# Attention on TensorE with another order of work inside a pair of heads, and the last 64 keys handled at full height

## The chip, the cores and the metric

One core of one Trainium2 chip runs the whole program. The metric is the device time of an execution in microseconds (us). The engines are named as in the profile: PE (TensorE matmul; PEld is its weight load), DVE (VectorE), ACT (ScalarE), POOL (GpSimd) and SP (SyncE, which here only issues DMA transfers).

## The reference, cut to what matters

Block-causal attention over 8 batches of 8 heads (576 positions, head size 64, blocks of 64), and then a mixture of 8 experts in which each of the 4608 tokens goes to its best expert alone.

```python
scores = scale * np.matmul(q, k.transpose(0, 1, 3, 2))
mask = block_i >= block_j                      # blocks of 64 positions
scores = np.where(mask, scores, -1000000000.0)
scores = scores - np.max(scores, axis=-1, keepdims=True)
attn = np.exp(scores)
attn = attn / (np.sum(attn, axis=-1, keepdims=True) + 1e-09)
x = np.matmul(attn, v)                         # to (4608, 512)
...
e_idx = np.argmax(x @ w_gate, axis=1)
for e in range(E):
    h = np.maximum(x[mask] @ w1[e], 0.0)
    out[mask] = gate_w[mask, None] * eom[mask, e, None] * (h @ w2[e])
```

## The kernel before

**Pairs.** Attention goes through 32 pairs of heads, p = 0 to 31; a batch is four pairs, and a unit of loading (u) is two pairs. In each round of the loop `advance(PLAN, p, ...)` three pairs are in flight. For pair p the softmax part runs: scores S0 to S4 on PE, one for each query tile (S0 to S3 are tiles of 128 queries, S4 the last 64 queries of both heads), their row maxima M0 to M4 on DVE, and the exponentials E0A to E4 on ACT, which also add up the row sums. For pair p-1 the probabilities are transposed: F0 to F5 are four fp32 transposes of 128x128 each on PE into a tile of `ps_t`, F6 is that of the last 64 keys, and C0 to C6 copy them to `pT` on ACT. For pair p-2 the values are multiplied in: V0 and V1 (the first 512 queries, into `ps_a`) and VM (the last 64 queries, into `ps_t`) on PE, X and XM copy the results to `xT` on ACT.

**What sets the order.** `PLAN` is a list of these names, written by hand, and each engine gets its instructions in the order of the list. PE keeps that order in all pairs; DVE and ACT keep it in pairs 1 to 27, and from pair 28 on a scheduler orders these two. A name with "-" (X-, E4-) is a piece that was left over from the round before. A "|" ends a turn: there the generators in `later` go one step on, which are the loads of the units to come, the finishing of a batch (`finish_batch`: reciprocals of the sums, the expert logits on PE, DVE and ACT, the routing tables) and `load_first` (the first expert's weights, from pair 28 on). Both lists have eight turns.

**Scores and their buffers.** The scores of tiles 0 and 1 of a pair share one buffer of `ps_s`, those of tiles 2, 3 and 4 take one each, and `ps_s` has two buffers. So S1 and S0 can start when the buffer of S3 has been read by E3A and E3B, S2 when that of S4 has been read by E4, S3 when that of S1 and S0 has been read by E1 and E0, S4 when E2 has read that of S2. `ps_t` has three buffers, `ps_a` one. In the list S0 stands behind M1, the maximum that DVE reads from the buffer into which S0 writes.

**The last 64 keys.** F6 transposes columns 512 to 575 of the last query tile's probabilities alone, to 64 rows; VM multiplies them by `v8`, the last 64 rows of V of both heads, as a product of height 64, behind four products of height 128.

**Loads.** A unit's q and k are fetched, split into two fp16 parts on POOL (`split`), transposed by two DMA transfers from SP's queue (`turn`), and then half swapped by two copies on DVE (`swap`, L115). Counted in turns from the start of the generator, `turn` comes at 8 and 9 and `swap` at 18 and 20, which for most units is in the pair just ahead of their first use. The last unit (15) is first used in pair 30; its generator starts in pair 26, one pair earlier than those of the others, and its `swap` comes at 13 and 14, in pair 27.

After pair 31 the mixture of experts runs, some 400 us of it, and the change does not touch it.

Of the kernel before, what the change touches and what calls it, by code (L numbers as in the profile page):

```python
# [20 lines left out]
P = 128  # L21
# [5 lines left out]
def block_attention_top1_moe(  # L27
# [56 lines left out]
    class Load:  # L84
# [26 lines left out]
        def swap(self, half):  # L111
            if half == 0:
                self.sw = sb.tile([P, MAXH * S], F16, name="sw")
            to, of = slice(64 * half, 64 * half + 64), slice(64 - 64 * half, 128 - 64 * half)
            nc.vector.tensor_copy(self.sw[to], self.res[0][of])  # L115

        def done(self):
            loaded[self.u] = (self.res[1], self.res[0], self.sw)

    def load_heads(u):  # L120

        x = Load(u)
        for i in range(2 if u == 2 else 0):
# [4 lines left out]
            lambda: x.turn(0), lambda: x.turn(1), lambda: x.swap(0), lambda: x.swap(1),  # L128
        )
        at = 0  # L130
        for t, do in zip((4, 5, 8, 9) + ((13, 14) if u == len(units) - 1 else (18, 20)), todo):
            while at < t:
                at += 1
                yield
            do()
        x.done()
# [5 lines left out]
    def load_start():  # L142
# [75 lines left out]
        nxt.turn(1)  # L218
        nxt.swap(0)
        nxt.swap(1)  # L220
        nxt.done()


    with tc.high_priority(offset=3000):
# [50 lines left out]
        nc.gpsimd.memset(wg_bd, 0.0)  # L275

# [6 lines left out]
    def constants():  # L283
# [15 lines left out]
        X- F0 S1 E4- M1 S0 | | C0 F1 F2 S2 M0 | C1 C2 E1A F4 M2 E1B E0A F3 E0B C4 C3 |  # L299
        V0 S3 F5 | E2A M3 E2B | VM C5 S4 XM E3A F6 E3B V1 | C6 M4 |  # L300
# [27 lines left out]
    def load_v(b, hp):  # L328
# [6 lines left out]
        v8 = sb.tile([64, 2, D], F32, name="v8", bufs=3)  # L335
        nc.sync.dma_start(v8, v[b, hA:hA + 2, 512:576, :].rearrange("h s d -> s h d"))
# [86 lines left out]
    def flip(probs, pT, copy):  # L423
# [31 lines left out]
        def turn_end():  # L455
            held[6] = ps_t.tile([P, 512], F32, name="ps_t")[0:64, 0:P]
            nc.tensor.transpose(held[6], probs[LAST][:, 512:S], ident)

        parts = {"F6": turn_end, "C6": lambda: copy(pT[0:64, 8 * TS:8 * TS + P], held[6])}
# [5 lines left out]
    def values(hp, pT, vs, v8, xT, copy):  # L465
# [651 lines left out]
    for p in range(B * NP):  # L1117
# [8 lines left out]
        while u not in loaded:  # L1126
            next(loads[2 * u - (4 if u == len(units) - 1 else 3)] if u else start, None)
# [34 lines left out]
    TAIL = " ".join(PLAN).replace("V1", "V1 X").split()  # L1162
# [115 lines left out]
```

## Time and profile before

| what | value |
|---|---|
| median of 3 runs | 828.63 us (830.1, 828.63, 825.52) |
| the profiled execution's own time | 818.4 us |
| its span | 816.7 us |
| PE busy | 750.4 us (92%) |
| DVE, ACT busy | 536.3 us (66%), 534.7 us (65%) |
| POOL busy | 320.5 us (39%) |

Shares of busy time are means over the program. The attention part reaches from the start to some 410 us and the experts' part from there to the end, so the stretches in the attention part have to be read by themselves.

### The profile page before, as it was taken

To read this page: it belongs to the slowest core of one execution; us is meant where nothing else is said; L and a number is where in the kernel's file an instruction comes from. 1 tells how busy PE (TensorE), PEld (TensorE's weight loads), DVE (VectorE), ACT (ScalarE), POOL (GpSimd) and SP (SyncE) were. 2 spreads that over 40 slices of the span, in tenths; PEclk is the share of its full clock that TensorE was granted. 3 is DMA by queue.
4 is the path that set the end of the run, shared out by engine and by line. 5 is a ranking of instruction groups with operands and counts; after the bars stand their busy time and mean duration, and the time that the engine had idled before them with its cause. 6 is when DMAs were issued, how large, how long until landed. Compare 5 with 4: busy or idle time off the path is not lost. (4 is left out here: it accounts for less than half of the span.)

```text
span 816.7 us, 18658 instructions
## 1 busy us (share of the span) xinstructions
PE 750.4 (92%) x6898; PEld 522.7 (64%) x6918; DVE 536.3 (66%) x1073; ACT 534.7 (65%) x1183; POOL 320.5 (39%) x445
## 2 busy tenths in 40 slices
PE   6799998999999998597979999999999999999994
PEld 3566666656666665465666775966669666686652
DVE  6556776767576776666563695867769676796530
ACT  4788787787878786576512686856568655785530
POOL 5668264463445460257224642322322243210001
PEclk9999999999999999898989999999999999999998
DMA  7889698957766365654117599699999969931601
GB/s 168 177 184 201 170 196 135 199 118 197 122 173 129 91 121 130 90 183 127 39 59 263 153 258 297 210 281 311 325 297 355 343 161 303 246 88 40 231 30 42
DMA packets 256629, 147.87 MB, mean 181 GB/s; under 512 B 224144, under 2 KB 224208, under 8 KB 256528
## 3 DMA queue, kind: packets, MB, share of 16 engines
q1 hardware_dynamic: 248416, 127.30, 60.7%
q0 software_dynamic: 8112, 19.29, 7.6%
q8 instruction: 56, 0.92, 0.5%
q14 instruction: 45, 0.37, 0.2%
HBM read 126.03 MB, written 19.34 MB: 178 GB/s over the span
## 5 line engine op out<-in xcount | busy, mean ns | idle before, releaser
L1009 PEld LDWEIGHTS <-w1b 128*128 128x128 f16 (+1 forms) x2208 | 177.7, 98 | 22.9 <-DVE w1b L886 1.3
L1009 PE MATMUL ps_s<-xt,w1b 128*128 128x256 f16 (+5 forms) x1920 | 175.2, 253 | 0.3 <-DVE w1b L886 0.3
L410 ACT ACTIVATE pt<-ps_s,nbs 128x512 f32<-128x512 f32 (+4 forms) x282 | 155.3, 569 | 17.2 <-DVE nbs L403 9.5
L1038 PE MATMUL ps_t<-w2b,hh 128*128 128x512 f16 (+1 forms) x540 | 162.4, 379 | 0.0
L395 DVE TENSOR_REDUCE nmx<-ps_s 128x2 f32<-128x1024 f32 (+1 forms) x125 | 102.9, 824 | 77.0 <-PE ps_s L380 76.4
L886 DVE TENSOR_TENSOR w2b<-w2f,w2b 128x1024 bf16<-128x1024 f32 x80 | 92.9, 1220 | 89.2 <-ACT w2b L884 88.9
L453 ACT COPY pT<-ps_t 128x512 f32<-128x512 f32 x181 | 102.2, 602 | 41.6 <-PE ps_t L444 41.6
L444 PE MATMUL ps_t<-ident,pt 128*128 128x128 f32 x768 | 112.0, 284 | 0.5 <-DVE xn L555 0.3
L1047 POOL DMA_INDIRECT out_dram<-ys,ids x38 | 49.6, 1306 | 160.0 <-ACT ys L1046 81.2
L1038 PE MATMUL ps_t<-w2b,hl 128*128 128x512 f16 x280 | 106.1, 379 | 1.1
L378 PE MATMUL ps_s<-tr,tr 128*128 128x512 f16 (+1 forms) x250 | 73.6, 307 | 35.8 <-DVE nmx L395 25.0
L1046 ACT ACTIVATE ys<-ps_t,ids 128x512 f32<-128x512 f32 (+1 forms) x38 | 26.1, 686 | 112.6 <-PE ps_t L1038 93.9
L444 PEld LDWEIGHTS ps_t<-ident,pt 128*128 128x128 f32 x768 | 85.9, 144 | 15.2 <-issue 4.3
L1038 PEld LDWEIGHTS <-hh 128*128 128x128 f16 x560 | 54.4, 98 | 62.0 <-issue 0.8
L886 DVE TENSOR_TENSOR w1b<-w1f,w1b 128x1024 bf16<-128x1024 f32 x80 | 92.8, 1217 | 1.4 <-ACT w1b L884 1.4
L103 POOL TENSOR_TENSOR sp<-nat,sp 128x320 f16<-128x320 f32 x120 | 87.5, 750 | 5.2 <-DVE sp L102 3.7
L102 POOL CAST sp<-nat 128x320 f16<-128x320 f32 x112 | 46.0, 438 | 97.4 <-DMA tr<-sp 82.2
L884 ACT CAST w1b<-w1f 128x1024 f16<-128x1024 f32 x80 | 78.3, 1045 | 2.6 <-DMA w1f<-in_moe_w_dram 2.6
L884 ACT CAST w2b<-w2f 128x1024 f16<-128x1024 f32 x80 | 77.8, 1043 | 1.5 <-DMA w2f<-in_moe_w_dram 1.5
L479 PE MATMUL ps_a<-pT,va 128*64 128x384 f32 (+2 forms) x256 | 74.6, 414 | 0.0
L479 PE MATMUL ps_a<-pT,vb 128*64 128x384 f32 (+2 forms) x256 | 74.6, 414 | 0.0
L379 PE MATMUL ps_s<-sw,tr 128*128 128x512 f16 (+1 forms) x250 | 73.4, 306 | 1.1 <-DVE sw L203 1.1
(218 smaller groups left out, 1181.8 us busy)
## 6 DMA issues: line engine op xcount, KB each, us to landing
w1f<-in_moe_w_dram SPq DMA_DIRECT2D x80, 512.0 KB
w2f<-in_moe_w_dram SPq DMA_DIRECT2D x80, 512.0 KB
nat<-in_k_dram SPq DMA_DIRECT2D x15, 576.0 KB
nat<-in_q_dram SPq DMA_DIRECT2D x15, 576.0 KB
x_d<-xn SPq DMA_DIRECT2D x32, 256.0 KB
va<-in_v_dram SPq DMA_DIRECT2D x32, 128.0 KB
vb<-in_v_dram SPq DMA_DIRECT2D x32, 128.0 KB
hh<-in_moe_w_dram SPq DMA_DIRECT2D x4, 512.0 KB
```

What stands on the lines that cost most here:

```text
L103: last_lo[0] = lo.tensor_tensor(sp[:, sl, 1, :], self.nats[i][:, sl], sp[:, sl, 0, :], ALU.subtract)
L378: nc.tensor.matmul(o, qq, k1[ab][:, 0:n], start=True, stop=False)
L379: nc.tensor.matmul(o, qq, k2[ab][:, 0:n], start=False, stop=False)
L395: nc.vector.tensor_reduce(nmx[:, t, :], at[t], AX.X, ALU.max, negate=True)
L410: last_exp[0] = nc.scalar.activation(probs[t][:, ab * n:(ab + 1) * n], at[t, ab], AF.Exp, bias=nbs[:, t, ab:ab + 1], scale=SCALE, accum_ou ...
L444: nc.tensor.transpose(held[i][:, P * j:P * j + P], probs[t][:, sl], ident)
L453: copy(to, ps)
L479: nc.tensor.matmul(pa[half, c0:512], vs[a][:, j, :], rows[:, a, j, c0 - P:512 - P], start=(j == 0), stop=(j == 3))
L884: nc.scalar.copy(hi, src)
L886: eng.tensor_tensor(lo[at], src[at], hi[at], ALU.subtract)
L1009: nc.tensor.matmul(ph[:, f4].rearrange("p (h n) -> p h n", n=w), wv[:, cc, f, :], xv[:, cc], start=(k == 0), stop=(k == 3 * KD - 1))
L1038: nc.tensor.matmul(py, hv[:, f, h], wv[:, f, :], start=(k == 0), stop=(k == 3 * KF - 1))
```

## The change

It has three parts.

1. `PLAN` is another list. On PE, S0 now follows S1 at once and M1 comes behind both; S2 comes behind F1 and F2 as before; F3 stands ahead of F4; F6 stands ahead of F5; V1 comes ahead of S4, and VM is last. On ACT, C0 comes ahead of the E4 of the pair before; C5 and C6 stand side by side ahead of E3; X and XM come last, in the round of their own values. The tail uses the same list as it is.
2. The last 64 keys are taken at full height: F6 transposes columns 448 to 575 (128x128, as the other transposes), C6 copies 128 rows, and `v8` has 128 rows, of which the upper 64 are zeros (written once, at the start, in three constant tiles that are used in turn), so that the last product of VM has height 128 as the others.
3. The last unit's swaps come at 18 and 20 like those of the others, which is in pair 28; the buffer of the swapped copy is taken with the second transpose; where a unit had to be loaded ahead of its pair by force, there is an assertion now.

```diff
     PLAN = """
-        X- F0 S1 E4- M1 S0 | | C0 F1 F2 S2 M0 | C1 C2 E1A F4 M2 E1B E0A F3 E0B C4 C3 |
-        V0 S3 F5 | E2A M3 E2B | VM C5 S4 XM E3A F6 E3B V1 | C6 M4 |
+        F0 S1 S0 M1 C0 | | E4- F1 C1 F2 M0 C2 E1A E1B E0A S2 E0B | F3 F4 C3 V0 S3 C4 |
+        M2 F6 F5 E2A E2B M3 | C5 C6 V1 S4 VM | E3A E3B X M4 | | XM
     """.split()
...
-    TAIL = " ".join(PLAN).replace("V1", "V1 X").split()
+    TAIL = list(PLAN)
...
+        v8s = [const.tile([P, 2, D], F32, name=f"v8{i}") for i in range(3)]
+        for v8 in v8s:
+            nc.gpsimd.memset(v8[0:64], 0.0)
...
-        v8 = sb.tile([64, 2, D], F32, name="v8", bufs=3)
-        nc.sync.dma_start(v8, v[b, hA:hA + 2, 512:576, :].rearrange("h s d -> s h d"))
+        v8 = v8s[(b * NP + hp) % 3]
+        nc.sync.dma_start(v8[64:128], v[b, hA:hA + 2, 512:576, :].rearrange("h s d -> s h d"))
...
-            held[6] = ps_t.tile([P, 512], F32, name="ps_t")[0:64, 0:P]
-            nc.tensor.transpose(held[6], probs[LAST][:, 512:S], ident)
+            held[6] = ps_t.tile([P, 512], F32, name="ps_t")[:, 0:P]
+            nc.tensor.transpose(held[6], probs[LAST][:, S - P:S], ident)
...
-        parts = {"F6": turn_end, "C6": lambda: copy(pT[0:64, 8 * TS:8 * TS + P], held[6])}
+        parts = {"F6": turn_end, "C6": lambda: copy(pT[:, 8 * TS:8 * TS + P], held[6])}
...
-                    if j < 4:
-                        nc.tensor.matmul(o, vs[a][:, j, :], rows[:, a, j, 512 - P:TS], start=(j == 0), stop=False)
-                    else:
-                        nc.tensor.matmul(o, v8[:, a, :], pT[0:64, 8 * TS + 64 * a:8 * TS + 64 * a + 64], start=False, stop=True)
+                    w, x = (vs[a][:, j, :], rows[:, a, j, 512 - P:TS]) if j < 4 else (v8[:, a, :], pT[:, 8 * TS + 64 * a:8 * TS + 64 * a + 64])
+                    nc.tensor.matmul(o, w, x, start=(j == 0), stop=(j == 4))
...
-        for t, do in zip((4, 5, 8, 9) + ((13, 14) if u == len(units) - 1 else (18, 20)), todo):
+        for t, do in zip((4, 5, 8, 9, 18, 20), todo):
...
-            lambda: x.turn(0), lambda: x.turn(1), lambda: x.swap(0), lambda: x.swap(1),
+            lambda: x.turn(0), lambda: (x.turn(1), x.done()), lambda: x.swap(0), lambda: x.swap(1),
...
-        while u not in loaded:
-            next(loads[2 * u - (4 if u == len(units) - 1 else 3)] if u else start, None)
+        assert u in loaded
```

**PE, the head of a pair.** L378 to L380 are a score's two products and its mask. Before, from the second half of S1 to S0:

```order
L378 MATMUL ps_s<-tr_2231,tr_2240 128x256
L379 LDWEIGHTS tr_2240
L379 MATMUL ps_s<-sw,tr_2240 128x256
L380 LDWEIGHTS mrow
L380 MATMUL ps_s<-mneg,mrow 128x64
L378 LDWEIGHTS tr_2240
L378 MATMUL ps_s<-tr_2231,tr_2240 128x128 [waits DVE_49]
L379 LDWEIGHTS tr_2240
L379 MATMUL ps_s<-sw,tr_2240 128x128
L380 LDWEIGHTS mrow
L380 MATMUL ps_s<-mneg,mrow 128x64
```

Now, the same place in the changed kernel, where the lines are L379 to L381:

```order
L379 MATMUL ps_s<-tr_2224,tr_2233 128x256
L380 LDWEIGHTS tr_2233
L380 MATMUL ps_s<-sw,tr_2233 128x256
L381 LDWEIGHTS mrow
L381 MATMUL ps_s<-mneg,mrow 128x64
L379 LDWEIGHTS tr_2233
L379 MATMUL ps_s<-tr_2224,tr_2233 128x128
L380 LDWEIGHTS tr_2233
L380 MATMUL ps_s<-sw,tr_2233 128x128
L381 LDWEIGHTS mrow
L381 MATMUL ps_s<-mneg,mrow 128x64
```

The first product of S0 (128x128) waited for DVE, that is for M1; it now waits for nothing, since M1 comes behind it.

**PE, the last keys.** L387 (L388) is S4, L457 (L458) F6, L444 (L445) the other transposes, L479 (L480) V1, and L549 a transpose of a batch's finishing. Before, from the end of S4:

```order
L387 MATMUL ps_s<-sw,tr_2240 64x64
L387 LDWEIGHTS tr_2240
L387 MATMUL ps_s<-sw,tr_2240 64x64
L457 MATMUL ps_t<-ident,pt_2738 64x128 [waits Activation_49]
L479 MATMUL ps_a<-pT,va 64x384
L479 MATMUL ps_a<-pT,vb 64x384
```

Now, from the end of S3 (L381 is its mask):

```order
L381 MATMUL ps_s<-mneg,mrow 128x64
L458 MATMUL ps_t<-ident,pt_2760 128x128 [waits DVE_49]
L445 MATMUL ps_t<-ident,pt_2760 128x128 [waits Activation_49]
L445 MATMUL ps_t<-ident,pt_2760 128x128 x3
L549 MATMUL ps_t<-ident,xT 128x128 [waits Activation_49]
L549 MATMUL ps_t<-ident,xT 128x128 x3
L480 MATMUL ps_a<-pT,va 64x384
L480 MATMUL ps_a<-pT,vb 64x384
```

F6 stood alone between S4 and V1, 64 rows high in its result; it now is 128 rows high and stands ahead of F5's four transposes, behind S3.

**ACT, from the end of one pair to the start of the next.** L410 (L411) are the exponentials, by their width: 512 is E3, 576 E4, 256 E1; L453 (L454) and L459 (L460) are the copies C0 to C5 and C6, and L493 (L492) X and XM. Before:

```order
L410 ACTIVATE pt_920,sums<-ps_s,nbs 128x512 [waits DVE_49] x2
L459 COPY pT<-ps_t 64x128 [waits PE_49]
L493 COPY xT<-ps_a 128x512 [waits PE_49]
L410 ACTIVATE pt_956,sums<-ps_s,nbs 128x576 [waits DVE_49,Activation_49]
L453 COPY pT<-ps_t 128x2x2x128 [waits PE_49,Activation_49]
L453 COPY pT<-ps_t 128x4x128 [waits PE_49] x2
L410 ACTIVATE pt_996,sums<-ps_s,nbs 128x256 [waits DVE_49]
```

Now:

```order
L411 ACTIVATE pt_931,sums<-ps_s,nbs 128x512 [waits DVE_49]
L492 COPY xT<-ps_a 128x512 [waits PE_49]
L492 COPY xT<-ps_t 128x64 [waits PE_49]
L454 COPY pT<-ps_t 128x2x2x128 [waits PE_49,Activation_49]
L411 ACTIVATE pt_972,sums<-ps_s,nbs 128x576 [waits DVE_49]
L454 COPY pT<-ps_t 128x4x128 [waits PE_49] x2
L411 ACTIVATE pt_989,sums<-ps_s,nbs 128x256 [waits DVE_49]
```

X stood ahead of E4 and now stands, with XM, behind E3 and ahead of C0, and E4 behind C0; C6 has 128 rows (and stands ahead of these rows, behind C5).

**DVE, around the last unit's swaps.** L115 (L113) are the two swaps, L395 (L396) the maxima M0 to M3 and L399 (L400) M4. Before:

```order
L453 COPY pT<-ps_t 128x2x2x128 [waits PE_49]
L395 TENSOR_REDUCE nmx<-ps_s 128x2 [waits PE_49]
L403 TENSOR_SCALAR nbs<-nmx 128x1 [waits DVE_49]
L403 TENSOR_SCALAR nbs<-nmx 128x1
L115 COPY sw<-tr_4981 64x2304 [waits DMAHW1_49]
L115 COPY sw<-tr_4981 64x2304
L399 TENSOR_REDUCE nmx<-ps_s 128x1
L687 COPY cnt_5178<-ps_t 128x8 [waits PE_49]
L403 TENSOR_SCALAR nbs<-nmx 128x1 [waits DVE_49]
L395 TENSOR_REDUCE nmx<-ps_s 128x2
```

Now:

```order
L396 TENSOR_REDUCE nmx<-ps_s 128x2
L703 SCALAR_TENSOR_TENSOR f_eq<-cnt_5153,f_mx,erev 128x8 [waits DVE_49]
L404 TENSOR_SCALAR nbs<-nmx 128x1 [waits DVE_49]
L404 TENSOR_SCALAR nbs<-nmx 128x1
L705 TENSOR_REDUCE f_er<-f_eq 128x1 [waits DVE_49]
L113 COPY sw<-tr_4960 64x2304 [waits DMAHW0_49]
L706 TENSOR_SCALAR first<-erev,f_er 128x8 [waits DVE_49]
L708 TENSOR_SCALAR f_e<-f_er 128x1
L396 TENSOR_REDUCE nmx<-ps_s 128x2 [waits PE_49]
L709 CAST f_i<-f_e 128x1 [waits DVE_49]
L113 COPY sw<-tr_4960 64x2304
```

The swaps stood right behind M1 of pair 28, ahead of M4 of the pair before (L399) and of M0; now they stand behind both, on either side of M2.

## Rows read from the trace of the kernel before

**Rows 1.** The page's first part: busy time, share of the span and instructions of each engine.

```profile
PE 750.4 (92%) x6898; PEld 522.7 (64%) x6918; DVE 536.3 (66%) x1073; ACT 534.7 (65%) x1183; POOL 320.5 (39%) x445
```

**Rows 2.** Two stretches of the attention part: start:end in us, length, then busy us and instructions of PE, PEld, DVE, ACT and POOL, the granted clock, the DMA engines' share and GB/s.

```profile
100.00:200.00 100.00, 91.97 (x935) 65.14 (x933) 70.63 (x195) 77.57 (x241) 49.79 (x85) 1.00 0.81 169
200.00:300.00 100.00, 92.73 (x939) 64.20 (x936) 69.07 (x194) 79.11 (x244) 51.03 (x88) 1.00 0.65 136
```

**Rows 3.** What PE waited for over the whole span: engine, its tile and line, the releaser, its tile and line: us in total, times, longest us.

```profile
PE ps_s L378 <- DVE nmx L395: 25.0, 31, 1.0
PE ps_s L378 <- ACT pt L410: 10.8, 8, 7.0
...
PE ps_t L564 <- ACT lgT L544: 4.0, 3, 2.6
```

**Rows 4.** The timeline of PE in pair 17, from its S1 to the S1 of pair 18: start us, us, engine, line, operation, tiles, shape of the tile of the array that is used and of the operands, count, and in brackets the idle time before it and its releaser. Matmuls overlap, so what a step costs is read from the starts. L378 to L380 at width 256, 128, 384 and 512 are S1, S0, S2 and S3, L387 is S4; L444 are the transposes F0 to F5, L457 is F6; L487 and L489 are VM, L479 V1.

```profile
205.91 0.27 PE L378 MATMUL ps_s<-tr,tr 128*128 128x256 f16 x1
...
206.37 0.19 PE L380 MATMUL ps_s<-mneg,mrow 128*128 128x64 bf16 x1
207.35 0.22 PE L378 MATMUL ps_s<-tr,tr 128*128 128x128 f16 x1 [0.78 <-DVE nmx L395]
...
207.63 1.07 PE L444 MATMUL ps_t<-ident,pt 128*128 128x128 f32 x8
208.53 0.33 PE L378 MATMUL ps_s<-tr,tr 128*128 128x384 f16 x1
...
211.27 0.39 PE L378 MATMUL ps_s<-tr,tr 128*128 128x512 f16 x1
...
212.17 0.19 PE L380 MATMUL ps_s<-mneg,mrow 128*128 128x64 bf16 x1
212.20 0.64 PE L444 MATMUL ps_t<-ident,pt 128*128 128x128 f32 x4
...
213.16 0.22 PE L487 MATMUL ps_t<-pT,va 128*64 128x64 f32 x1
...
213.22 0.22 PE L487 MATMUL ps_t<-pT,va 128*64 128x64 f32 x1
...
213.38 0.33 PE L489 MATMUL ps_t<-pT,v 64*64 64x64 f32 x4
213.64 0.41 PE L387 MATMUL ps_s<-tr,tr 128*64 128x512 f16 x2
...
214.12 0.20 PE L387 MATMUL ps_s<-sw,tr 128*64 128x64 f16 x2
214.25 0.30 PE L457 MATMUL ps_t<-ident,pt 128*64 128x128 f32 x1
214.48 0.54 PE L479 MATMUL ps_a<-pT,va 128*64 128x384 f32 x1
...
215.93 0.66 PE L444 MATMUL ps_t<-ident,pt 128*128 128x128 f32 x4
216.42 0.27 PE L378 MATMUL ps_s<-tr,tr 128*128 128x256 f16 x1
```

**Rows 5.** The timeline of ACT in the same pair: E4 of the pair before, the copies C1 and C2, E1A, and the copies C4 and C3.

```profile
206.04 0.75 ACT L410 ACTIVATE pt<-ps_s,nbs 128x576 f32<-128x576 f32 x1
...
208.30 1.08 ACT L453 COPY pT<-ps_t 128x512 f32<-128x512 f32 x2 [0.85 <-PE ps_t L444]
209.26 0.49 ACT L410 ACTIVATE pt<-ps_s,nbs 128x256 f32<-128x256 f32 x1
...
210.85 1.10 ACT L453 COPY pT<-ps_t 128x512 f32<-128x512 f32 x2
```

**Rows 6.** The timeline of DVE in the same pair, M1 alone.

```profile
206.60 0.69 DVE L395 TENSOR_REDUCE nmx<-ps_s 128x2 f32<-128x512 f32 x1 [1.14 <-PE ps_s L380]
```

**Rows 7.** Timelines of four engines: on PE the S1 of pairs 1, 28 and 29 and the S2 of pair 28, on DVE M1's last step in pair 28 and the last unit's two swaps (L115), on ACT the E4 behind them, and on SP the two transposes that the swaps wait for.

```profile
22.69 0.27 PE L378 MATMUL ps_s<-tr,tr 128*128 128x256 f16 x1 [0.69 <-ACT pt L410]
...
334.20 5.18 SPq L108 DMA_TRANSPOSE tr<-sp  x2
...
336.21 0.27 PE L378 MATMUL ps_s<-tr,tr 128*128 128x256 f16 x1
...
337.74 0.21 DVE L403 TENSOR_SCALAR nbs<-nmx 128x1 f32<-128x1 f32 x2
342.78 1.52 DVE L115 COPY sw<-tr 64x2304 f16<-64x2304 f16 x2 [4.83 <-DMA tr<-sp]
...
345.30 0.74 ACT L410 ACTIVATE pt<-ps_s,nbs 128x576 f32<-128x576 f32 x1 [5.43 <-DVE nbs L403]
...
346.18 0.48 PE L378 MATMUL ps_s<-tr,tr 128*128 128x384 f16 x1 [7.05 <-ACT pt L410]
...
356.27 0.27 PE L378 MATMUL ps_s<-tr,tr 128*128 128x256 f16 x1
```

**Rows 8.** PE's logits in pair 30, from the timeline, and the stretch around them, from the table of stretches (columns as in rows 2).

```profile
372.71 1.12 PE L564 MATMUL ps_t<-ident,lgT 128*128 128x128 f32 x4 [2.63 <-ACT lgT L544]
...
371.00:376.00 5.00, 3.29 (x15) 2.89 (x16) 1.38 (x2) 3.67 (x13) 5.00 (x9) 0.53 0.82 227
```

More of the change, by code (lines that the diff above doesn't have):

```diff
@@ L111, in swap @@
         def swap(self, half):
-            if half == 0:
-                self.sw = sb.tile([P, MAXH * S], F16, name="sw")
             to, of = slice(64 * half, 64 * half + 64), slice(64 - 64 * half, 128 - 64 * half)
@@ L117, in done @@
         def done(self):
+            self.sw = sb.tile([P, MAXH * S], F16, name="sw")
             loaded[self.u] = (self.res[1], self.res[0], self.sw)
@@ L135, in load_heads @@
             do()
-        x.done()
     units = [(b, h0, 4) for b in range(B) for h0 in (0, 4)]
@@ L218, in load_start @@
         nxt.turn(1)
+        nxt.done()
         nxt.swap(0)
         nxt.swap(1)
-        nxt.done()
     with tc.high_priority(offset=3000):
```

## The prediction

> **What bounds the kernel now.** I read the busy shares by stretch first. Over the program PE is busy 92% and ACT and DVE 65% [rows 1]; inside the attention part, from 100 to 300 us, it is PE 92 to 93%, ACT 78 to 79%, DVE 69 to 71% [rows 2]. So PE is the bound there, with some 7 to 8 us of idle in each 100 us and little else to take away. Next I read what PE waited for: one line stands out, the first score product waiting for the maximum (line L395), 25.0 us in 31 waits, 0.8 us each, and then one single wait of 7.0 us for an exponential [rows 3]. The 31 waits are one a pair. The timeline of pair 17 shows the place [rows 4]: S1 starts at 205.91, its last product at 206.37, and S0 at 207.35, 0.78 us of it idle until DVE has finished M1, which takes 0.69 us from 206.60 [rows 4, 6]. S0 writes into the buffer that M1 reads. The pair ends with the next S1 at 216.42, so it lasts 10.51 us. From pair 1 to pair 28, S1 to S1, it is (336.21 - 22.69) / 27 = 11.61 us [rows 7]; the 1.10 us above pair 17 are the finishing steps of batches that share the engines. The experts' part isn't touched, so all of the change lies in the first 410 us.
>
> **The sum** is made for the profiled execution (818.4 us) and then put on the median.
>
> (a) **S0 ahead of M1.** Before, S0's first product came 207.35 - 206.37 = 0.98 us behind S1's last; where nothing waits, a last score product is followed after 0.03 us (212.17 to 212.20) [rows 4]. That is 0.95 us a pair, and pairs 1 to 27 have it: 27 x 0.95 = 25.6 us off. (All waits of this line sum to 25.0 us as idle time, which is the modelled end's lower reading [rows 3].) The wait can go only if nothing else comes as late. What is late next, counted from S1 = 0 with the durations of pair 17: S0 ends at 0.48 + 0.28, F1 and F2 take 0.90, so PE wants S2 at 1.66, and S3 2.74 us later, at 4.40 [rows 4]. S2 needs the buffer that E4 of the pair before reads. ACT now does C0 first: F0 ends at about 0.17 (215.93 + 0.66 against 216.42), C0 takes half of the 0.96 us of two copies, so E4 starts near 0.68; in pair 28, S2 started 0.88 us behind E4 [rows 4, 5, 7]. That gives 1.56: free by 0.10 us. S3 needs E0B: E4 0.75, two copies 0.96, E1 and E0 together 210.85 - 209.26 = 1.59, so it ends near 4.0 and S3 may go at 4.2, free by 0.2 us [rows 5]. M1, which now starts behind S0, at about 0.97, is followed by E1 only at 2.4, so its 0.69 us are covered by E4 and the copies. S4 needs E2, done near 6.1, and PE comes to S4 at about 7.35: free by 1.2 us. The margins at S2 and S3 are thin, and this is the first rival below.
>
> (b) **The last keys at full height, and the new neighbours on PE.** The last ordinary product of VM comes at 213.22, one pair of products lasts 213.22 - 213.16 = 0.06, the half-height ones come at 213.38 and S4 at 213.64 [rows 4]. In one shape the way from 213.22 to 213.64 would be three steps of 0.06, not 0.42: about 0.25 us less. S4's last product comes at 214.12 and V1, behind the lone F6, at 214.48: 0.36 us for one transpose; in a row of eight one takes 0.90 / 8 = 0.11 [rows 4]. F6 now stands in front of F5's four: 0.25 us less. Against it stand new neighbours, V1 to S4 and S4 to VM, which no row shows; a step without and with a change of shape costs 0.03 (212.17 to 212.20) and 0.16 (213.22 to 213.38) [rows 4], so together up to 0.2 us, less what the old neighbours (F5 to VM, V1 to F0) give back. Net 0.30 to 0.50; I take 0.40, nearer to the rows of equal shape since V1, S4 and VM all have 64 columns: 27 x 0.40 = 10.8 us off (8 to 13.5). C6 copies 128 rows in place of 64, on ACT, which isn't the bound; the two products of height 128 have no more columns than before. The rows show pauses of 0.10 us more where the tile's shape goes from 128x64 to 64x64 [rows 4]. The Trainium skill, TensorEngine Tiling (Array Packing), "Key Properties", says that a change of the tiling mode drains the engine; the trace agrees in that place, but F6 and V1 have one mode and yet cost 0.36 us, so by that rule alone the term would be 27 x 0.25 = 6.8 us.
>
> Put together from its pieces the new pair takes: S1 0.48, S0 0.28, F1 and F2 0.90, S2 to V0 2.74, S3 0.93, F6 and F5 five times 0.11, V1 1.45, S4 0.61, VM ten times 0.06, F0 0.49 [rows 4]. That is 9.0 us, against 10.51 - 0.95 - 0.40 = 9.16 by the two terms.
>
> (c) **Finishing steps** put more copies on ACT in three pairs of four, 1.10 us a pair on PE. Where such a copy falls ahead of E4 or E0B, the thin margins are used up. I take 0.3 us once in each of seven batches: +2 us (0 to +5). X, in its own round now, has its buffer free long before the next V0; that costs nothing.
>
> (d) **Pair 28.** It lasts 356.27 - 336.21 = 20.06 us. DVE stood at the swap from 337.95 until the transpose landed, 4.83 us, then did both swaps and only then M4 of pair 27; E4 waited for that, S2 for E4, 7.05 us [rows 7]; the transposes had started at 334.20, so the first landed 8.58 us later. Now M4, M1 and M0 stand ahead of the swap and M2 behind it. The transposes wait for the scores that read the buffer before (S4 of pair 27) and, in SP's queue, for the store into `v8`, which waits for VM, now last in its pair: I put their start about 1 us before S1 of pair 28. If they land again after 8.6 us, at 7.6, M2 comes near 8.4 instead of 2.6, E2 ends near 10.7, and S4 waits 3.5 us. If they land by 4 us, E2 is not late, since ACT comes to it only at 5. So pair 28 takes 9.16 + 1.10 + (0 to 3.5) = 10.3 to 13.8; the one row that there is stands at the upper end, I take 13.0: 7 us off (6.3 to 9.8).
>
> (e) **Pairs 29 to 31 and the tail.** The scheduler orders DVE and ACT here. Three pairs with (a) and (b) would give 3 x 1.35 = 4 us; the weights' casts on ACT come earlier in the row, ahead of an E4, 1 us each at most: 3 us off (0 to 8). The upper end is the 2.63 us wait for the logits behind a cast and the granted clock of 0.53, near the lower of its two levels, in the 5 us around it [rows 8]. Three fills with zeros on POOL at the start, and the old tail's order: 0.
>
> Sum: -25.6 - 10.8 + 2 - 7 - 3 = -44.4, so 774 for the profiled execution. The median of the runs lies 828.63 - 818.4 = 10.2 us above it, and I find no reason for that to change: 784. With all terms at their good ends it is 772, with all at their bad ends 794.
>
> **Rivals.**
> 1. **The margins at S2 and S3 fail.** `ps_s` has two buffers, and S2 and S3 now hang on ACT's E4 and E0B. If the copies and exponentials run 0.3 us later each than in pair 17 (ACT is 78% busy and would be near 90% in the shorter pair [rows 2]), PE waits 0.6 to 0.9 us a pair, and 16 to 24 us come back: 800 to 808. For it: margins of 0.1 and 0.2 us, and finishing steps on ACT in most pairs. Against it: ACT has 78 us of work in 100 us, that is 9.0 us in a pair of 11.61 us, and PE without the wait still needs 10.3. ACT is not the bound, it is only a matter of order.
> 2. **The whole wait moves.** If E4 behind C0 makes S2 as late as M1 made S0, (a) is nothing and (b), hidden behind the wait, too; (d) and (e) remain: 818. If also the last unit's swap stops DVE as before, with M2 behind it, the change is not to be seen: 826. For it: the two chains are of the same kind, a maximum or an exponential between two scores in one buffer. Against it: E4 starts by 0.68 in the pair, M1 ended at 1.4.
> 3. **Slower: the swaps stop DVE in every unit.** The transposes of a unit now start some 1 us later, behind VM and its `v8` load, and the swap is due in the next pair but one, some 12 to 13 us on in the shorter pairs, where 8.58 us were needed in pair 28 [rows 7]. If they land later than that, DVE stands there with M2 behind it in all 14 units, as once before. A delay of 4.83 us in each would be 14 x 4.83 = 68 us: 852; it turns the gain into a loss from (833 - 784) / 14 = 3.5 us a unit, that is from a landing about 16 us after the start. [...]
> 4. **Half height is cheaper.** By the widths of the rows the two products of VM should not last longer at full height. The Trainium skill, TensorEngine Tiling (Array Packing), "When to Use Tiling", asks for row tiling at a height of 64 or less, which is what the change takes away. As a mechanism here: the two half-height products would lose 0.06 us each and the new neighbours cost the full 0.16 twice, so (b) is nothing: 784 + 11 = 795. The four half-height records took 213.38 to 213.64, 0.26 us, where the full ones take 0.06 a step [rows 4]; the trace speaks against the rule in this place.
>
> **How the numbers follow.** Forecast (784) 0.60; half height cheaper (795) 0.07; margins fail (800 to 808) 0.19; the wait moves: 818 0.04, 826 0.04; slower 0.06. A measurement of this kernel can tell about 0.5%, which is 824.5 to 832.8. Faster is 0.60 + 0.07 + 0.19 + 0.04 = 0.90, same 0.04, slower 0.06. The range is from 772, the forecast's lower end, to 808, the upper end of rival 1; what is left out is the 0.14 of the cases above it and a little of the forecast.
>
> **What would show it.** In the trace after: S0's first product 0.03 us behind S1's last and no wait for L395 on PE (a); S1 to S1 near 9.2 us in plain pairs and about 10.3 in the mean; the last product of VM 0.06 us behind the one before, and V1 0.03 to 0.1 us behind F5 (b); PE's waits for exponentials at S2 and S3 under 0.1 us a pair, or rival 1; DVE's wait for the swap only once, in pair 28, and pair 28 at 10 to 14 us (d). The forecast is wrong if PE's idle share between 100 and 300 us stays at 7 to 8%, or if V1, S4 and VM next to each other cost more than 0.2 us at their seams.

## The result, and the profile after

| kernel | median of its runs | ratio to the kernel before, with its 95% interval |
|---|---|---|
| before | 827.08 us (822.65 to 830.1, 4 runs) | |
| changed | 791.02 us (787.7 to 796.78, 4 runs) | 0.9576 (0.9502 to 0.9649) |
| changed again, on the chip of e5 to e8 (e6) | 792.74 us | 0.9580 (0.9550 to 0.9611) |
| changed again, on the chip of e9 to e12 (e10) | 793.7 us | 0.9603 (0.9556 to 0.9651) |

The changed kernel is 4% faster, 36.1 us by the medians. 784 us were forecast, with a range of 772 to 808. Its profiled execution took 791.47 us, with a span of 789.6 us.

The two stretches, which answer to [rows 2]:

```profile
100.00:200.00 100.00, 94.54 (x982) 67.82 (x982) 73.51 (x203) 81.68 (x256) 56.33 (x95) 0.98 0.89 183
200.00:300.00 100.00, 93.96 (x998) 67.60 (x996) 74.29 (x207) 83.22 (x256) 48.01 (x81) 1.00 0.65 135
```

PE's waits in these 200 us, first of the kernel before and then of the changed one (columns as in rows 3; "issue" marks idle time in which PE waited for nothing that the profile shows):

```profile
PE ps_s L378 <- DVE nmx L395: 13.3, 17, 0.8
PE ps_s L378 <- ACT pt L410: 1.4, 4, 0.8
```

```profile
PE ps_s L379 <- ACT pt L411: 6.0, 4, 1.9
PE ps_s L380 <- issue: 1.4, 2, 0.9
```

PE's waits for the maximum, 25.0 us over the span before, are gone. But PE's share between 100 and 300 us rose only from 92 to 94%, from 15.3 to 11.5 us of idle time. The waits for the maximum were 13.3 us of it. In their place S3 waits 6.0 us for exponentials where it waited 1.4, four times as before but longer, and 4.7 us are pauses marked "issue", on which the last section has more. The timeline of PE in pair 3, which answers to [rows 4], shows what an undisturbed pair looks like:

```profile
42.09 0.27 PE L379 MATMUL ps_s<-tr,tr 128*128 128x256 f16 x1
...
42.56 0.19 PE L381 MATMUL ps_s<-mneg,mrow 128*128 128x64 bf16 x1
42.59 0.22 PE L379 MATMUL ps_s<-tr,tr 128*128 128x128 f16 x1
...
47.44 0.31 PE L458 MATMUL ps_t<-ident,pt 128*128 128x128 f32 x1
...
49.35 0.27 PE L480 MATMUL ps_a<-pT,va 128*64 128x128 f32 x1
...
49.46 0.39 PE L388 MATMUL ps_s<-tr,tr 128*64 128x512 f16 x2
...
49.92 0.20 PE L388 MATMUL ps_s<-sw,tr 128*64 128x64 f16 x2
49.95 0.25 PE L488 MATMUL ps_t<-pT,va 128*64 128x64 f32 x1
...
50.39 0.22 PE L488 MATMUL ps_t<-pT,va 128*64 128x64 f32 x1
...
50.45 0.29 PE L488 MATMUL ps_t<-pT,v 128*64 128x64 f32 x4
50.66 0.66 PE L445 MATMUL ps_t<-ident,pt 128*128 128x128 f32 x4
51.16 0.27 PE L379 MATMUL ps_s<-tr,tr 128*128 128x256 f16 x1
```

S0 starts 0.03 us behind S1's last product (42.56, 42.59). The seams V1 to S4 (49.35 to 49.46, the width of the last V1 product) and S4 to VM (0.03) cost nothing. S1 to S1 is 51.16 - 42.09 = 9.07 us, where 10.51 stood before.

The steps that finish a batch reach over three pairs, and the second of these (pair 7, then 11, 15, 19 and 23) gives its gain back. Timelines of DVE, ACT and PE in pair 7, whose S1 starts at 81.25 (L396 are M1 and M0; L554 and L592 are two of the seven finishing steps of DVE between them, which scale the batch's values and choose the experts; L411 is E1A, L379 S3):

```profile
82.60 0.68 DVE L396 TENSOR_REDUCE nmx<-ps_s 128x2 f32<-128x512 f32 x1
...
83.52 0.68 DVE L554 TENSOR_TENSOR xn<-ps_t,rec 128x512 f32<-128x512 f32 x1
...
85.75 0.41 DVE L592 TENSOR_TENSOR oh<-er,erev 128x40 f16<-128x40 f32 x1
...
86.31 0.42 DVE L396 TENSOR_REDUCE nmx<-ps_s 128x2 f32<-128x256 f32 x1
...
86.77 0.47 ACT L411 ACTIVATE pt<-ps_s,nbs 128x256 f32<-128x256 f32 x1 [2.56 <-DVE nmx L396]
...
88.55 0.38 PE L379 MATMUL ps_s<-tr,tr 128*128 128x512 f16 x1 [1.94 <-ACT pt L411]
```

M0 starts 3.0 us behind M1's end, since these steps stand between them; E1 waits 2.56 us for it and S3 1.94 us for E0B. The pair takes 12.80 us; before it took 13.17. In the kernel before M0 stood behind the same steps; these are DVE's M0, E1A on ACT and S3 on PE in its pair 7, whose S1 starts at 88.22:

```profile
93.14 0.42 DVE L395 TENSOR_REDUCE nmx<-ps_s 128x2 f32<-128x256 f32 x1
...
93.60 0.48 ACT L410 ACTIVATE pt<-ps_s,nbs 128x256 f32<-128x256 f32 x1 [1.48 <-DVE nmx L395]
...
95.38 0.38 PE L378 MATMUL ps_s<-tr,tr 128*128 128x512 f16 x1 [0.86 <-ACT pt L410]
```

So M0 comes 4.92 us behind S1 before and 5.06 after, and S3 7.16 and 7.30: without the wait for M1, S3 comes no sooner in such a pair.

At the end of attention, pair 28 takes 327.27 - 314.90 = 12.4 us, and pair 30 still 20.15 (19.48 before). Timelines of DVE, SP, ACT and PE, which answer to [rows 7, 8]:

```profile
319.61 0.76 DVE L113 COPY sw<-tr 64x2304 f16<-64x2304 f16 x1 [2.07 <-DMA tr<-sp]
...
338.94 0.38 SPq L923 DMA_DIRECT2D hh<-in_moe_w_dram  x1
...
342.48 1.04 ACT L883 CAST w2b<-hh 128x1024 f16<-128x1024 f32 x1 [4.28 <-DMA hh<-in_moe_w_dram]
344.90 1.12 PE L563 MATMUL ps_t<-ident,lgT 128*128 128x128 f32 x4 [4.61 <-ACT lgT L543]
```

DVE waits 2.07 us for the swap where it waited 4.83. In pair 30 ACT stands in the first cast of the second weight matrix until the weights land, 3.5 us behind their issue, and the logits' copies, for which PE waits, stand behind that cast.

### The profile page after: what moved, and what is told of

Same layout as the page of the kernel before. It is cut to its first block, busy times and chain, and to the rows that moved or that the text cites. A ratio compares the mean times of both kernels' runs of the same rounds, so it can differ in the third digit from the quotient of the medians.

```text
span 789.6 us, 18680 instructions
## 1 busy us (share of the span) xinstructions
PE 732.1 (93%) x6898; PEld 517.2 (66%) x6918; DVE 535.5 (68%) x1073; ACT 532.7 (67%) x1183; POOL 327.1 (41%) x448
## 5 line engine op out<-in xcount | busy, mean ns | idle before, releaser
L411 ACT ACTIVATE pt<-ps_s,nbs 128x512 f32<-128x512 f32 (+4 forms) x282 | 155.4, 570 | 17.8 <-DVE nmx L396 11.8
L396 DVE TENSOR_REDUCE nmx<-ps_s 128x2 f32<-128x1024 f32 (+1 forms) x125 | 102.4, 820 | 50.2 <-PE ps_s L381 43.5
L454 ACT COPY pT<-ps_t 128x512 f32<-128x512 f32 x180 | 101.2, 601 | 29.7 <-PE ps_t L445 26.9
L1046 POOL DMA_INDIRECT out_dram<-ys,ids x38 | 54.9, 1445 | 156.4 <-ACT ys L1045 70.4
L445 PE MATMUL ps_t<-ident,pt 128*128 128x128 f32 x768 | 110.5, 281 | 4.4 <-ACT xT L492 2.7
L445 PEld LDWEIGHTS ps_t<-ident,pt 128*128 128x128 f32 x768 | 86.5, 143 | 13.1 <-ACT lgT L543 4.2
L379 PE MATMUL ps_s<-tr,tr 128*128 128x512 f16 (+1 forms) x250 | 72.6, 306 | 12.7 <-ACT pt L411 12.3
L480 PE MATMUL ps_a<-pT,va 128*64 128x384 f32 (+2 forms) x256 | 75.0, 416 | 0.0
L480 PE MATMUL ps_a<-pT,vb 128*64 128x384 f32 (+2 forms) x256 | 75.0, 416 | 0.0
L380 PE MATMUL ps_s<-sw,tr 128*128 128x512 f16 (+1 forms) x250 | 70.8, 305 | 3.6 <-issue 1.4
```

Source lines behind the costliest of these rows:

```text
L379: nc.tensor.matmul(o, qq, k1[ab][:, 0:n], start=True, stop=False)
L380: nc.tensor.matmul(o, qq, k2[ab][:, 0:n], start=False, stop=False)
L396: nc.vector.tensor_reduce(nmx[:, t, :], at[t], AX.X, ALU.max, negate=True)
L411: last_exp[0] = nc.scalar.activation(probs[t][:, ab * n:(ab + 1) * n], at[t, ab], AF.Exp, bias=nbs[:, t, ab:ab + 1], scale=SCALE, accum_ou ...
L445: nc.tensor.transpose(held[i][:, P * j:P * j + P], probs[t][:, sl], ident)
L454: copy(to, ps)
```

## The experiments

They ran on three chips: e1 to e4 where the kernel before took 816.42 us, e5 to e8 where it took 828.88, e9 to e12 where it took 828.29. Times are therefore compared as ratios, and pairs by their S1 to S1. A plain pair is one without finishing steps.

**e1, half height in the new order.**

```diff
-            nc.tensor.transpose(held[6], probs[LAST][:, S - P:S], ident)
+            nc.tensor.transpose(held[6], probs[LAST][:, 512:S], ident)
...
-(v8[:, a, :], pT[:, 8 * TS + 64 * a:...])
+(v8[:, a, :], pT[0:64, 8 * TS + 64 * a:...])
```

> The changed kernel with the last 64 keys at half height again (64 rows of F6, C6 and v8, last product of VM of height 64), the new list kept. Theory (the term b is real and comes from both edits): plain pairs last 9.05 + 0.25 to 0.40 = 9.3 to 9.5 us from S1 to S1 where the changed kernel has 9.05 to 9.1, the whole 7 to 12 us longer than the changed kernel, some 798 to 803. The half-height products are again followed by a gap of 0.26 us before the next PE work and F6 costs over 0.2 us. Rival 1 (all of b came from the new order on PE, the height gives nothing): plain pairs 9.05 to 9.1, the whole at 791. Rival 2 (the zeros' height costs): plain pairs under 9.05.

Measured: 781.39 us, ratio 0.9572 (0.9546 to 0.9597), which is the changed kernel's ratio; plain pairs 9.17 to 9.21 us. PE at the two places of the half height, in pair 3:

```profile
46.94 0.28 PE L455 MATMUL ps_t<-ident,pt 128*64 128x128 f32 x1
47.05 0.60 PE L442 MATMUL ps_t<-ident,pt 128*128 128x128 f32 x4
...
49.86 0.22 PE L485 MATMUL ps_t<-pT,vb 128*64 128x64 f32 x1
50.01 0.33 PE L485 MATMUL ps_t<-pT,v 64*64 64x64 f32 x4
50.27 0.66 PE L442 MATMUL ps_t<-ident,pt 128*128 128x128 f32 x4
```

F6 at half height costs 0.11 us in its new place (47.05 - 46.94), no more than a full one (0.14 in pair 3 of the changed kernel). The product of VM costs 50.27 - 49.86 = 0.41, against 50.66 - 50.39 = 0.27 at full height. So the height gives 0.12 to 0.14 us a pair, between the theory and rival 1; that is 3 to 4 us, and too little for the ratios to tell.

**e2, M1 between S1 and S0 again.**

```diff
-        F0 S1 S0 M1 C0 | | E4- F1 ...
+        F0 S1 M1 S0 C0 | | E4- F1 ...
```

> The changed kernel with M1 between S1 and S0 again, and nothing else moved. Theory (term a): S0 waits about 0.78 us for M1 in every pair, plain pairs last 9.05 + 0.95 = 10.0 us, 27 pairs give 25 us, some 812 to 816. Rival (the shorter pair runs into the next bound anyway, so that the wait was only the first of two): the pauses that PE has in five pairs without a named releaser (0.8 to 1.3 us each in pairs 10, 14, 17, 21 and 26) and the 1.9 us waits of S3 for E0B in pairs 7, 11, 15, 19 shrink by as much as S0 waits, plain pairs 10.0 but finishing pairs only 0 to 0.5 us longer: some 804 to 808.

Measured: 800.9 us, ratio 0.9824 (0.9794 to 0.9853). Plain pairs last 10.00 us, 0.94 more. PE's wait for M1 over the span:

```profile
PE ps_s L379 <- DVE nmx L396: 28.2, 31, 1.5
```

The second finishing pairs take 12.55 to 13.19 us, about what they take in the changed kernel (12.78 to 12.80 in pair 7 and 11.8 to 14.4 in the others, in three profiles); S3's waits there shrink to 0.20, 0.84, 0.21, 0.21 and 0.21 us while S0's come. Against the changed kernel's 0.958 to 0.960 the wait costs some 0.023 x 816 = 19 us, between the two expectations: the theory holds in plain pairs, the rival in the second finishing ones. None of the pauses without a named releaser showed in the four profiles of this chip, with the wait or without.

**e3, M0 right behind M1.**

```diff
-        F0 S1 S0 M1 C0 | | E4- F1 C1 F2 M0 C2 ...
+        F0 S1 S0 M1 M0 C0 | | E4- F1 C1 F2 C2 ...
```

> The changed kernel with M0 right behind M1 on DVE, ahead of the finishing steps that the turns put between them, and nothing else moved. Theory (in the second finishing pair of a batch, DVE's steps stand between M1 and M0, so E1 and E0 come late and S3 waits for the buffer): the waits of S3 in pairs 7, 11, 15, 19, 23 (1.94, 1.94, 1.21, 1.89, 0.96 us) fall under 0.3 us, these pairs last 10.9 to 11.2 us instead of 11.8 to 12.8, the whole is 6 to 9 us shorter, some 782 to 785. Rival (ACT's own work is what makes E0B late there): S3 waits as before, no change, 791. Second rival (DVE is the bound of these pairs: 12.1 us busy of 12.8): the wait moves to S4 or to the next pair's S1, a gain under 3 us.

Measured: 775.93 us, ratio 0.9518 (0.9479 to 0.9558), 0.6 to 0.9% better than the changed kernel, and 5.5 us below e1 and e4, which have the changed kernel's ratio on this chip. Of the waits of S3 in those pairs none is left; the pairs take 12.49, 11.66, 11.24, 12.05 and 11.58 us, not the 10.9 to 11.2 of the theory. On DVE M2 now stands behind the finishing steps, as the timeline of ACT in pair 7 shows (this is E2):

```profile
88.89 0.58 ACT L411 ACTIVATE pt<-ps_s,nbs 128x384 f32<-128x384 f32 x1 [3.01 <-DVE nbs L404]
```

PE waits only 0.22 us of that, at S4, and 0.55 and 0.28 us for finishing steps of DVE; in the other four pairs what is left is 0.2 us at S4, in pair 19 also 0.40 for DVE. So DVE's order was the cause of S3's waits, not ACT's work. Pair 30 took 22.37 us here and gave back part of the gain: ACT's cast waited 6.6 us for the weights.

**e4, the last unit's swaps in pair 27 again.**

```diff
-        for t, do in zip((4, 5, 8, 9, 18, 20), todo):
+        for t, do in zip((4, 5, 8, 9) + ((13, 14) if u == len(units) - 1 else (18, 20)), todo):
```

> The changed kernel with the last unit's two swaps at turns 13 and 14 again, in pair 27, and nothing else moved. Theory (term d: the swap on DVE in front of M4 of pair 27 is what stopped pair 28): DVE waits 4 to 6 us for the transpose again, S2 of pair 28 waits some 5 to 7 us for E4, pair 27 or 28 is 6 to 8 us longer, the whole some 797 to 799. Rival (the new list alone lets M4 pass, the turn of the swap doesn't matter): within 2 us of the changed kernel.

Measured: 781.39 us, ratio 0.9568 (0.9539 to 0.9596): no difference. Yet the stall came back, as DVE and PE in pair 28 and PE in pair 30 show:

```profile
318.12 0.76 DVE L113 COPY sw<-tr 64x2304 f16<-64x2304 f16 x1 [5.18 <-DMA tr<-sp]
...
320.79 0.48 PE L379 MATMUL ps_s<-tr,tr 128*128 128x384 f16 x1 [8.29 <-ACT pt L411]
...
343.60 0.66 PE L563 MATMUL ps_t<-ident,lgT 128*128 128x128 f32 x4 [0.71 <-ACT lgT L543]
```

Pair 28 took 20.24 us, and pairs 29 and 30 only 10.00 and 15.09. From S1 of pair 28 to S1 of pair 31 it is 45.33 us, against 44.07, 43.55 and 47.09 in e1 to e3 on the same chip. The theory is right on the stall and wrong on the total: the stall hid the wait for the weights.

**e5, S0 ahead of M1 in the old list, alone.**

```diff
-        X- F0 S1 E4- M1 S0 | | C0 ...
+        X- F0 S1 S0 E4- M1 | | C0 ...
```

> The kernel before with one edit to its list: S0 right behind S1, and M1 behind the E4 of the pair before (S1 S0 E4- M1 in place of S1 E4- M1 S0); half height, the old order of F6, V1, S4 and VM and the old turns of the last unit's swaps stay. Theory (term a stands by itself, and b's order is the rest of the pair's gain): plain pairs last 10.51 - 0.95 = 9.55 us, which with 0.39 us for the order of F6, V1, S4 and VM and 0.12 for the height makes the 9.06 of the changed kernel; 27 pairs give 20 to 26 us. Rival (in the old list E4 stands behind X, which needs V1, so S2 comes too late without the wait): plain pairs 9.8 to 10.3, waits of S2 for E4 of 0.3 to 0.7 us a pair, 6 to 18 us.

Measured: 806.59 us, ratio 0.9748 (0.9719 to 0.9777), 22.3 us. Plain pairs 9.57 us, and S2 waits in none of them. The theory holds: 0.94 us of the 1.45 are the wait for M1, and it takes one moved word; E4 stands behind X here as before, so the new order on ACT is not needed for it.

**e6, the changed kernel again**, unchanged.

> The changed kernel as it is, once more, beside the others. Theory (the pauses of PE without a named releaser in pairs 10, 14, 17, 21 and 26, 5 us in all, belong to that one execution and not to the order of the work, since none of the four variants showed them): no such pauses, pair 10 in 10.8 to 11.4 us, the ratio to the kernel before again 0.955 to 0.960, and the trace's span some 5 us shorter against its kernel before than the first. Rival (they belong to the full height together with the order S1 S0): pauses in the same five pairs, 0.7 us each, twice a pair.

Measured: ratio 0.9580, span 789.8 us, and the pauses are there, in pairs 10, 14, 17, 21 and 25. So the theory falls: they don't belong to one execution. All four kernels on this chip had them, e5 with the old list too (pairs 9, 13, 17, 21 and 25 of 11.4 to 11.6 us for 9.57), so the rival falls as well.

**e7, the second matrix's casts four turns later.**

```diff
-        for w, fn, r0, r1 in ((w1, split_w1, 8, 1), (w2, split_w2, 4, 2)):
+        for w, fn, r0, r1 in ((w1, split_w1, 8, 1), (w2, split_w2, 8, 2)):
```

> The changed kernel with the casts of the first expert's second weight matrix four turns later (the wait of 4 turns ahead of them is 8), nothing else moved. Theory (pair 30 stands because ACT takes the first of these casts ahead of the logits' copies and then waits for its weights, 4.3 us, and PE for the logits, 4.6 us, with the clock at half behind it): the wait of PE for the logits falls under 1 us, pair 30 lasts 12 to 15 us instead of 20, the attention part ends 5 to 8 us sooner. Rival (the weights come late in any case, and the casts' lateness only moves the wait to the experts' part): the gain in pair 30 is given back there, the whole within 2 us of the changed kernel.

Measured: 791.44 us, ratio 0.9535 (0.9476 to 0.9595). The wait for the logits is 0.71 us and pair 30 takes 14.54; but pairs 28 and 29 took 14.39 and 12.84, and S1 of pair 28 to S1 of pair 31 lasts 41.77 us, against 43.51, 45.08 and 41.09 in three profiles of the changed kernel. Its interval holds the changed kernel's 0.958: not decided.

**e8, both.** The edits of e3 and e7 together.

> The changed kernel with both M0 right behind M1 and the second matrix's casts four turns later. Theory (two separate waits, in the second finishing pairs and in pair 30): the gains add up, some 5 us of the first and 5 to 8 of the second, ratio to the kernel before 0.940 to 0.945. Rival (with M0 early pair 30 stood at 22.4 us for the same weights, so that part of the first gain was lost there, and the load of the weights is the bound of pairs 28 to 31): ratio 0.947 to 0.952, S1 of pair 28 to the end of pair 31 no shorter than with M0 early alone.

Measured: 781.28 us, ratio 0.9445 (0.9406 to 0.9485), 11.5 us below the changed kernel on the same chip. S3 waits in none of the second finishing pairs, and S1 of pair 28 to S1 of pair 31 lasts 40.85 us, against 47.09 in e3. That is the theory's number, and the lowest ratio of the study; that the two gains add up is not shown by it, since that of e7 was not decided.

**e9, the kernel before itself**, unchanged, with a profile.

> The kernel before, unchanged, with a profile of this chip. In the first four experiments the kernel before took 816.4 us and in the next four, on another chip, 828.9, and the profile of the kernel before (818.4 us) shows none of the pauses of PE behind the batches' scatters that all four of the later profiles show. Theory (the two chips differ by those pauses, so the profile of the kernel before and that of the changed kernel are of different kinds): where the kernel before takes near 829 us, its pairs 9, 13, 17, 21 and 25 are 1.5 to 2.5 us longer than the 10.51 us of the first profile, with pauses just behind the last scatter of a batch, 10 us in all; where it takes near 816, there are none. Rival (pauses come only without the wait for M1): none on either chip, and the 12 us are spread over the program.

Measured: 829.45 us, span 827.9. Pairs 9, 13, 17, 21 and 25 take 12.97, 11.30, 11.34, 11.30 and 11.24 us where the first profile has 10.51 in each, and pair 10, with a mean granted clock of 0.77, 15.05 for 12.28: 8.4 us more in these six. Behind the scatter in pair 9 PE's pause is a wait of the next S1 for E3; SP starts a transpose in the same moment as ACT its E3A, 2 us behind the start of the last scatter, and DVE, idle for 3.51 us, its M4 at 124.73:

```profile
122.65 0.91 POOL L645 DMA_INDIRECT tab_d<-idg,sli  x1 [0.30 <-issue]
...
124.68 3.04 SPq L108 DMA_TRANSPOSE tr<-sp  x1
...
124.72 0.69 ACT L410 ACTIVATE pt<-ps_s,nbs 128x512 f32<-128x512 f32 x1
...
126.22 0.27 PE L378 MATMUL ps_s<-tr,tr 128*128 128x256 f16 x1 [2.30 <-ACT pt L410]
```

The theory holds: the two first profiles, of the kernel before and of the changed one, were of different kinds, and the pauses need no change of the list.

**e10, the changed kernel beside it**, unchanged.

> The changed kernel, unchanged, beside the one before on the same chip. Theory: on a chip with the pauses 791 to 794 us with pairs 10, 13 or 14, 17, 21 and 25 longer by 0.7 to 2.5 us; on one without them 780 to 784 us, none of these pauses, and a gain of 33 to 36 us, of which 27 pairs give 30 to 33.

Measured: 793.7 us, span 788.9, with the pauses. S1 of pairs 1, 28, 29 and 31 on PE, of the kernel before (e9) and of the changed one (e10):

```profile
22.12 0.27 PE L378 MATMUL ps_s<-tr,tr 128*128 128x256 f16 x1 [0.69 <-ACT pt L410]
...
344.72 0.27 PE L378 MATMUL ps_s<-tr,tr 128*128 128x256 f16 x1
...
364.77 0.27 PE L378 MATMUL ps_s<-tr,tr 128*128 128x256 f16 x1
...
395.00 0.27 PE L378 MATMUL ps_s<-tr,tr 128*128 128x256 f16 x1
```

```profile
22.95 0.27 PE L379 MATMUL ps_s<-tr,tr 128*128 128x256 f16 x1 [0.69 <-ACT pt L411]
...
314.99 0.27 PE L379 MATMUL ps_s<-tr,tr 128*128 128x256 f16 x1 [0.21 <-ACT pt L411]
...
327.82 0.27 PE L379 MATMUL ps_s<-tr,tr 128*128 128x256 f16 x1
...
356.08 0.27 PE L379 MATMUL ps_s<-tr,tr 128*128 128x256 f16 x1
```

Pairs 1 to 27 lost 322.60 - 292.04 = 30.6 us, pair 28 20.05 - 12.83 = 7.2, pairs 29 and 30 30.23 - 28.26 = 2.0; the first S1 comes 0.8 us later, and from S1 of pair 31 on nothing changed (432.9 and 432.8 us). That makes the 39.0 us between the spans. The profiled execution of e10 is the fastest of its four (790.79 us, median 793.7); by the medians e9 and e10 differ by 35.8 us.

**e11, full height in the old list, alone.** The edits of the change to F6, C6, `v8` and VM in the kernel before.

> The kernel before with the last 64 keys at full height and nothing else (the old list, the old swaps). Theory (in the old list the half-height product stands between VM's others and S4, so it costs 0.25 us there, and the lone F6 at half height stands between S4 and V1 with 0.36 us, of which full height changes little): the step from VM's last ordinary product to S4 falls from 0.42 to 0.17 us, the pair from 10.51 to 10.2 to 10.4 us, 4 to 9 us in all, ratio 0.989 to 0.995. Rival (the wait for M1 takes nothing of it, but a new change of shape between the full F6 and V1 costs what is saved): 10.5 us a pair, ratio 0.997 to 1.003.

Measured: 823.71 us, ratio 0.9930 (0.9904 to 0.9957); pairs of 10.27 us. PE from VM to V1 in pair 2:

```profile
41.05 0.22 PE L490 MATMUL ps_t<-pT,vb 128*64 128x64 f32 x1
...
41.22 0.39 PE L390 MATMUL ps_s<-tr,tr 128*64 128x512 f16 x2
...
41.68 0.20 PE L390 MATMUL ps_s<-sw,tr 128*64 128x64 f16 x2
41.81 0.33 PE L460 MATMUL ps_t<-ident,pt 128*128 128x128 f32 x1
42.07 0.54 PE L482 MATMUL ps_a<-pT,va 128*64 128x384 f32 x1
```

VM's last ordinary product to S4 is 0.17 us instead of 0.42, the theory's figure, and S4 to V1 around the lone F6 is 0.39, full or half (0.36).

**e12, the scatter four turns later.**

```diff
-        for fn in (excess, shares, gather, gate, do(weights, scatter)):
+        for fn in (excess, shares, gather, gate, do(weights)):
             yield fn
+        for i in range(4 if b < B - 2 else 0):
+            yield do()
+        yield scatter
```

> The changed kernel with the scatter of the routing table of batches 0 to 5 four turns (about half a pair) later, nothing else moved. Theory (the pauses of PE hang on the scatter): on a chip with the pauses they move with it, to about 0.4 to 1.7 us behind the new last scatter of each batch, and keep their size; the time stays within 3 us of the changed kernel. Rival (they hang on PE's own place in its instruction stream, for example the short products of VM): they stay in pairs 10, 14, 17, 21 and 25 at the same place of the pair. On a chip without pauses nothing is to be seen.

Measured: 799.35 us, ratio 0.9619 (0.9562 to 0.9677). The edit did not do what it was for. The last scatters of the first five batches start 8.98 us into pair 9, 8.82 into pair 13, 7.83 into 17, 7.81 into 21 and 0.43 into 26; in e10 they start 1.15 into pair 10, 0.45 into 14, 7.85 into 17, 7.91 into 21 and 9.20 into 25, so two came sooner, two stayed, and one came 0.5 us later. The pauses stand 0.6 to 2.2 us behind each. Inconclusive.

## Why the prediction was right, point by point

| term | forecast | from S1 to S1, e9 against e10 |
|---|---|---|
| (a) and (b), plain pairs | -36.4 | 27 x (10.51 - 9.06) = -39.2 |
| (c) given back, mostly in finishing pairs | +2 | 39.2 - 30.6 = +8.6 |
| (d) pair 28 | -7 | -7.2 |
| (e) pairs 29 to 31 | -3 | -2.0 |
| start | 0 | +0.8 |
| sum | -44.4 | -39.0 |

By the medians the gain was 36.1 us, by these two profiles 39.0; the sum had 44.4, and (c) makes most of the difference.

**(a)** was right in mechanism and size: 0.95 forecast, 0.94 in e2 and in e5. The thin margins at S2 and S3 held in plain pairs, so neither the first nor the second rival came there. The third didn't come either: DVE waited for a swap's transpose in pair 28 alone (2.07 us in the first profile after, 5.13 and 3.07 in e6 and e10).

**(b)** was forecast as 0.40 and is 0.51 us a pair, but with other shares. With 0.94 for the wait, the height gives 0.12 in the new list and 0.24 in the old one (e1, e11), the order the rest, 0.39 or 0.27. The 0.25 for the half-height product was right where it was read, between VM and S4; in the new list VM is followed by F0, which uses another shape of the array than VM at either height, and the height gives only 0.41 - 0.27 = 0.14 there. The 0.25 for F6 came from its place alone and not from its height: 0.11 us at half height in front of F5, 0.39 at full height between S4 and V1. The new seams, for which up to 0.2 us were set aside, cost nothing. The rival that half height is cheaper fell: full height with zeros is 0.12 to 0.24 us a pair cheaper here. The Trainium skill, TensorEngine Tiling (Array Packing), "When to Use Tiling", asks for row tiling at a height of 64; these pairs go the other way.

**(c)** is the step that was mis-sized: "I take 0.3 us once in each of seven batches: +2 us (0 to +5)". 8.6 us were given back, and the mean pair takes 292.04 / 27 = 10.82 us where "about 10.3" was expected. Pair by pair, 7.6 us of it lie in the five second finishing pairs, which gained nothing; 2.4 us lie in pairs 26 and 27, and 1.3 us in pair 4, where S1 waits 1.1 us for DVE's swap, which the sum did not have. Against that, pair 1 gained 1.5 us more than a plain one, and the pairs with pauses took 1.0 us less. I had looked for ACT's copies ahead of E4 and E0B and, on DVE, at M1 alone, "followed by E1 only at 2.4"; M0 is not in the margins. But E1A starts 0.04 us behind the end of M0, in both kernels, although its own maximum is M1's, which was done more than 3 us sooner; why it waits for M0 is open. DVE's finishing steps stand between M1 and M0, hold E1 up by that, and S3 behind it (1.94 us in pair 7). With M1 between S1 and S0 most of that time was hidden in S0's wait, as e2 shows. e3 and e8 show the cause: with M0 behind M1 the wait of S3 is gone, the five pairs take 59.0 and 56.5 us together where they take 62.1 to 63.9 in three profiles of the changed kernel, and the ratio falls. So the first rival's place, S3 behind E0B, was right, in five pairs, but with DVE and not ACT as the cause.

**(d)** came as forecast (13.0 for pair 28; 12.37, 15.24 and 12.83 in three profiles), yet e4 shows that the moved swaps are not worth it: without them pairs 28 to 30 take 45.3 us on a chip where variants with them take 43.6 to 47.1. What the stall in pair 28 costs comes back in pair 30, whose casts wait for the weights. The 7.2 us of the table are thus not what the third part of the change is worth. **(e)** was therefore too hopeful where its step said "3 us off (0 to 8)" with the logits' wait as the upper end: that wait was 4.61 us in the first profile after and 0.71 in e10, of the same kernel. Pairs 29 and 30 take 31.14, 29.85 and 28.26 us in three profiles of it and 30.14 and 30.23 in two of the kernel before, so no gain there is clear of the spread.

**The median.** The sum was put on 828.63 us with "I find no reason for that to change" for the 10.2 us between the profiled execution and the median. There was a reason: the profile before shows none of the pauses that the same kernel has in e9, so the two first profiles differ by 27.1 us in span while e9 and e10 differ by 39.0. The changed kernel has the pauses in some executions too (spans of 788.9 to 789.8 us with them, and 781.6 and 782.2 in its variants e1 and e4 without), so the sum stood on the right base, but by luck: nothing that the prediction read told it so.

## What to carry to other kernels

When a wait between two engines is taken out of a short repeated loop, look for what the waited-for engine did in that time: here DVE had its side work there, and a fifth of the pairs' gain (7.6 of 39.2 us) went back to it; putting the next maximum ahead of that work won part of it back. Cost an edit of shape by its neighbours on both sides, since the same half-height product cost 0.25 us in front of S4, which has the shape of the products before it, and 0.14 in front of F0, which has not. A stall near a load that the next stage waits for may be worth nothing, as e4 shows: time from the stall to the end of that stage, not the stall.

## What the runs showed that was not expected

In the first profile of the changed kernel, and on the chips of e5 to e8 and of e9 to e12 in every profile, there is a pause of about 0.7 us, or a few of them, behind the start of a batch's last scatter: 0.3 to 2 us behind it in the new list, up to 3.6 us in the old, where PE's pause is mostly a wait for E3. In e10, on PE (the stretch behind the scatter of 113.51 us):

```profile
113.86 0.32 PE L537 MATMUL ps_t<-xT,wg_bd 128*32 128x64 f32 x4 [0.49 <-issue]
114.61 0.24 PE L537 MATMUL ps_t<-xT,wg_bd 128*32 128x64 f32 x1 [0.43 <-issue]
```

In the four profiles of e1 to e4, on the third chip, and in the first profile of the kernel before, there is none. By e9 against that first profile they, with the lowered clock behind one of them, make up some 8 of the 12 us by which the kernel before differs between the chips (816.42 and 828 to 829). In e9 ACT, DVE and SP stood with PE, so it need not be PE's own. The scatters fall at different places of the pair (8.98 us into it or 1.81, for example, in e8), and the pauses go with them, so PE's own place in its list is not what makes them. But the other finishing steps move with the scatter, and the run meant to move it alone did not do so: that they hang on the scatter itself is not shown, and their cause stays open.
